# Filler products behind the last parts of w2, one eviction on another engine, and the flag's sums at a later place

## The chip, the cores and the metric

The kernel runs on one core of one Trainium2 chip. The metric is device time in microseconds (us) of one execution. Engines are named as in the profile: PE is TensorE (PEld its weight loads), DVE is VectorE, ACT is ScalarE, POOL is GpSimd, SP is SyncE, which issues all DMAs here.

## What is computed

The reference chains three layers over 4608 tokens (8 sequences of 576, 512 features): an attention through 32 memory slots, a soft mixture of 8 experts, and a last layer whose weights come as float64.

```python
x = attention(q, k, v, phi)                 # (4608, 512)
logits = x @ moe_phi                        # 32 slots
d = softmax(logits, over tokens); slot_input = d.T @ x
for e in range(8):                          # 4 slots per expert
    slot_out[e] = relu(slot_input[e] @ w1[e]) @ w2[e]
c = softmax(logits, over slots)
x = c @ slot_out
h = x @ w_in                                # 512 -> 2048
g = h - tanh(h)
out = g @ w_out                             # 2048 -> 512
```

The kernel replaces the last layer by a low-order form in the slot weights. A validity flag is computed beside it; where the flag says that the form would not be accurate enough, a general branch at the end recomputes the layer. With these inputs the branch is not taken into the general part.

## The kernel before

Every instruction stands in an order written out by hand. Two strings, `ORDER` for the attention and `TAIL` for all behind it, name small operations; the kernel emits them in that order, and each engine gets its own instructions in the order in which they are emitted. Only semaphores between engines move the time at which they run. All loads and stores are issued by SyncE: loads in one fixed sequence, each as soon as the page of SBUF that it overwrites has been given back.

The part that the change touches, with the names in `TAIL`:

- `a2.0` to `a2.15` and `a2.b` (function `a2_half`, line 1299): sixteen parts of w2, 1 MB each, multiplied as they land. Each part is 8 matrix products of 32 x 256, in four column groups of TensorE, accumulated in two PSUM banks. A float32 product counts as two instructions in the trace, so a part is x16 there. Each part that is done gives its page back, and a load of w_out follows into it.
- `nB`, `D2` (lines 1211, 1215): a small product of the validity flag between `a2.13` and `a2.14`.
- `so`, `sT`, `sC` (lines 1328 to 1338): the result of w2 is copied by ScalarE and VectorE, turned by four products and copied again.
- `ft0` to `ft3` (line 1352): the slot outputs times the decoded w_in, 32 x 256 products into four banks named `hS`; `hs` copies them (line 1364), `st` turns them (line 1371, tile `hp`).
- `tt`, `hc`, `gs`, `gz`, `G` (lines 1387 to 1415): powers of the result, and the factor tiles `G` on VectorE.
- `da`, `db`, `dc` (lines 950, 954, 958): three VectorE passes that turn a part of w_in or w_out from float64 words into float32; `ck` (line 964, ScalarE) sums what the flag needs; `rd` (line 1238) rounds.
- `L`, `M`, `or`, `Ra`, `Rb`, `Rc`, `Rd` (lines 1437 to 1501): the two halves' right-hand sides `R`, from `G`, w_out and the rows.
- `k0.b`, `u0.b`, then `k1.b`, `u1.b` for b from 0 to 17 (lines 1527, 1545): the output products of the first and of the second half of the columns, and their evictions from PSUM. A last letter V or A says whether VectorE or ScalarE evicts. Four banks take turns. Two evictions fill a transfer of 512 KB; the first and last of a half are 256 KB.
- `fs` (lines 1556 to 1559): four VectorE sums of the flag. `fB`, `fm`, `fw`, `fo`, `fb` (lines 1564 to 1585) finish the flag at the very end; all engines load it and branch (line 1601).

In `TAIL` of before, `fs` stands behind `u0.13A`; on VectorE that is behind the last decoding pass (`dc.wout.6`) and ahead of `u0.14V`.

Of the kernel before, what the change touches and what calls it, by code (L numbers as in the profile page):

```python
# [189 lines left out]
q3 h1.2 q4 h1.3 q5 ck.win.1 mh1 h1.4 h1.5 h1.6 h1.7 ms r0 cB r1 hT q6 dc da.win.5 rl z1 z0 sp0 sq0 cT sq2 tp0 sp1 a2.0  # L190
tp1 tc1 a2.1 tc0 tp2 stk db.win.5 a2.2 da.win.4 sq3 sq1 tp3 a2.3 da.win.6 tc2 lg0 tc3 tp4 tp5 lg1 a2.4 lg3 a2.5
db.win.4 tc5 lg2 da.win.7 tc4 a2.6 dc.win.5 z2 z3 cX a2.7 db.win.6 sp2 sp3 tp6 a2.8 da.wout.0 tp7 da.wout.1 tc7 a2.9
tc6 tp8 dc.win.4 db.wout.0 dc.win.6 ck.win.5 tc8 n3 tp9 nT n5 a2.10 tp10 db.wout.1 tc9 db.win.7 tp11 a2.11 ck.win.6
dc.win.7 ck.win.4 dc.wout.0 a2.12 a2.13 nB dc.wout.1 D2 a2.14 rd.0A a2.15 ck.win.7 a2.b so0 so1 sT0 sT1 sC0 sC1 ft0
tc10 da.wout.2 db.wout.2 ft1 rd.1A ft3 mgz dc.wout.2 hs0A st0 tc11 hs1A st1 ck.wout.0 tt0 da.wout.3 hc0 db.wout.3 ft2
gs0 gz0 G0.0 G0.1 da.wout.4 hs3A hs2A rd.2A ck.wout.2 st3 M0.0 st2 tt1 dc.wout.3 L01.1 L00.1 L01.0 gs1 hc1 gz1 rd.3P
L00.0 M0.1 M0.3 ck.wout.1 ck.wout.3 M0.2 o40A G1.1 G1.0 ss0 db.wout.4 L00.3 dc.wout.4 or0 ss1 Ra00A Ra01A L00.2 L01.2
Rb000A Rc00 L01.3 Rb001A Rb010A rd.4P k0.0 Rc01 da.wout.5 db.wout.5 k0.1 da.wout.6 k0.2 u0.0A k0.3 Rd00 Rd01 u0.2A
u0.1A u0.3A k0.4 M1.0 k0.5 k0.6 k0.7 u0.5A u0.4V k0.8 k0.9 u0.6A k0.10 Rb011A da.wout.7 L11.0 u0.7A db.wout.7 k0.11
u0.8A u0.9A k0.12 u0.10A L10.0 dc.wout.7 k0.13 M1.3 k0.14 u0.12A db.wout.6 dc.wout.5 u0.11A k0.15 dc.wout.6 k0.16  # L200
rd.6P u0.13A fs M1.1 k0.17 rd.5A M1.2 L10.1 u0.14V u0.17V ck.wout.7 o41A rd.7P L10.2 or1 u0.15A u0.16A L10.3 L11.2
Ra10V Rb100A Rc10 k1.0 Ra11V Rb101V Rc11 u1.0A Rd10 k1.1 k1.2 k1.3 k1.4 u1.1A ck.wout.5 k1.5 u1.2V u1.3V k1.6 u1.4V
L11.3 L11.1 u1.5A k1.7 u1.6V k1.8 u1.7V Rb110A k1.9 Rb111A Rd11 k1.10 u1.8A k1.11 k1.12 ck.wout.4 u1.9V u1.12A u1.10V
k1.13 u1.11V u1.13V k1.14 u1.14V k1.15 fB k1.16 k1.17 ck.wout.6 u1.16V fm fw fo fb u1.15A u1.17A
"""

ORDER = """
# [22 lines left out]
def tile_kernel(  # L230
# [13 lines left out]
    NP, P, NI, H, M = phi.shape[0], 128, 9, kv.shape[2], phi.shape[3] // kv.shape[2]  # L244
# [19 lines left out]
    mm = nc.tensor.matmul  # L264
# [3 lines left out]
    ident = cst.tile([P, P], F32, name="ident")  # L268
# [30 lines left out]
    def view(off, shape, dtype=F32):  # L299
        n = 1  # L300
        for d in shape[1:]:
            n *= d
        o, e, t = [x for x in lots if x[0] <= off][-1]
        assert off % 4 == 0 and off + 4 * n <= e, (off, shape)
        v = t[0 : shape[0], (off - o) // 4 : (off - o) // 4 + n]
        if dtype != F32:
            v = v.bitcast(dtype)
        if len(shape) > 2:
            names = "abcdefg"[: len(shape) - 1]
            v = v.rearrange(  # L310
                f"p ({' '.join(names)}) -> p {' '.join(names)}", **{c: d for c, d in zip(names[:-1], shape[1:-1])}
            )
        return v
# [103 lines left out]
    for w in PLAN.split():  # L417
        n, p = w.split(":")
        n, j = n.split(".")
# [438 lines left out]
    def op(name):  # L858
        def keep(f):
            T[name] = f  # L860
            return f

        return keep
# [14 lines left out]
    @op("ms0")  # L878
    def _():
        G.memset(siM, 0.0)  # L880
# [111 lines left out]
    def bank(j, name):  # L992
        return ps.tile([P, 512], F32, tag=f"bank{j}", name=name)
# [8 lines left out]
    n3 = sc_[:, 360 : 360 + NP]  # L1002
    n4 = sc_[0:NP, 364:366]
    n5 = sc_[0:NP, 368 : 368 + B].rearrange("p (r b) -> p r b", r=NP)
    D2 = sc_[:, 376 : 376 + B]
# [15 lines left out]
    dc = view(13 * PG, [P, NP, NI, NSL])  # L1021
# [269 lines left out]
    a2 = []  # L1291
# [52 lines left out]
    hS, hp = {}, {}  # L1344

    def feat_ops(k):
        @op(f"ft{k}")
        def _():
            hS[k] = bank(2 + k, "hS").rearrange("p (a x) -> p a x", a=2)
            for g in (2 * k, 2 * k + 1):  # L1350
                for kc in range(4):
                    mm(  # L1352
                        hS[k][32 * kc : 32 * kc + 32, g % 2],
                        soT[:, kc],
                        wf[g][:, kc],
                        start=True,
                        stop=True,
                    )

        for e_, c_ in (("V", V.tensor_copy), ("A", A.copy)):  # L1360

            @op(f"hs{k}{e_}")
            def _(c_=c_):
                c_(hSs[k], hS[k])

        @op(f"st{k}")
        def _():
            if k // 2 not in hp:
                hp[k // 2] = bank(6 + k // 2, "hp")[:, 0 : 8 * XW].rearrange("p (c x) -> p c x", x=XW)
            for c in range(4):  # L1370
                mm(
                    hp[k // 2][:, 4 * (k % 2) + c],
                    hSs[k][:, c // 2, (c % 2) * P : (c % 2) * P + P],
                    stkx,
                    start=True,
                    stop=True,
                )

    for k in range(4):
        feat_ops(k)  # L1380

    def curve_ops(k):
        c = slice(8 * k, 8 * k + 8)

        @op(f"tt{k}")
        def _():
            A.activation(out=tt_[:, c], in_=hp[k][:, :, NSL:], func=AF.Square)

        @op(f"hc{k}")
        def _():  # L1390
            A.copy(hc[:, c], hp[k][:, :, NSL:])

        @op(f"ss{k}")
        def _():
            A.activation(out=ss[:, c], in_=hp[k][:, :, 0:NSL], func=AF.Square)

        @op(f"gs{k}")
        def _():

            t = tt_[:, c]  # L1400
            V.scalar_tensor_tensor(out=gs[:, c], in0=t, scalar=-1.5, in1=t, op0=ALU.add, op1=ALU.mult)

        @op(f"gz{k}")
        def _():
            t = tt_[:, c]
            G.tensor_scalar(out=g2[:, c], in0=t, scalar1=-2.0 / 15.0, scalar2=1.0 / 3.0, op0=ALU.mult, op1=ALU.add)
            G.tensor_tensor(out=g2[:, c], in0=g2[:, c], in1=t, op=ALU.mult)
            G.tensor_tensor(out=gz[:, c, 0:B], in0=hc[:, c], in1=g2[:, c], op=ALU.mult)

        for j in range(2):  # L1410

            @op(f"G{k}.{j}")
            def _(j=j):
                b = slice(4 * j, 4 * j + 4)
                V.tensor_tensor(
                    out=curves(f"G{k}")[:, :, b],
                    in0=hp[k][:, :, 0:NSL].unsqueeze(2).to_broadcast([P, 8, 4, NSL]),
                    in1=gs[:, c, b].unsqueeze(3).to_broadcast([P, 8, 4, NSL]),
                    op=ALU.mult,
                )  # L1420
# [88 lines left out]
    n = 0  # L1509
# [174 lines left out]
```

## Time and profile before

| | us |
|---|---|
| median of 3 runs | 243.46 (242.02 to 244.72) |
| the profiled execution, its own time | 245.09 |
| span of its trace | 243.1 |
| busy in the span: PE, DVE, ACT, POOL | 179.4, 162.3, 99.0, 77.8 |
| DMA: moved, mean rate | 93.56 MB, 385 GB/s |

All times below are counted from the start of the span. The own time is 2.0 us more than the span, and the profiled execution is 1.6 us above the median of the runs.

### The profile page before, as it was taken

What the parts mean: (1) busy time and instruction counts of PE and PEld (TensorE: products, weight loads), DVE (VectorE), ACT (ScalarE), POOL (GpSimd) and SP (SyncE); (2) the same over time, 40 slices, a digit from 0 to 9 for tenths busy, and PEclk for the clock granted to TensorE, in tenths of its full rate; (3) what the DMA queues carried; (4) which work ended last, traced back from release to release, by engine and by line L of the source; (5) the groups of instructions that cost most, each with busy time, mean ns of one, the idle gap of its engine ahead of it and who ended that gap; (6) DMA issues with size and microseconds to landing.
All of it is one profiled execution on the core that took longest, in us unless ns stands there. A gap on an engine that the chain in (4) does not pass through costs nothing.

```text
span 243.1 us, 6355 instructions
## 1 busy us (share of the span) xinstructions
PE 179.4 (74%) x2657; PEld 126.3 (52%) x2657; DVE 162.3 (67%) x246; ACT 99.0 (41%) x192; POOL 77.8 (32%) x139
## 2 busy tenths in 40 slices
PE   0368299886998998857975986991757799878920
PEld 0255287665677777645552326550323467665720
DVE  1594649962587954862968999433496279999940
ACT  2131610851545355352341160120433359786930
POOL 4001148876573774331021034760000005404000
PEclk9999959999999999995599997699789679999975
DMA  6999999999999999999999999999999992086993
GB/s 248 425 414 417 422 419 416 415 417 420 420 416 409 422 421 423 419 425 427 431 426 417 406 418 430 425 426 429 423 426 425 426 426 96 21 358 269 393 419 113
DMA packets 17459, 93.56 MB, mean 385 GB/s; under 512 B 1936, under 2 KB 2064, under 8 KB 10768
## 3 DMA queue, kind: packets, MB, share of 16 engines
q1 hardware_dynamic: 17424, 93.09, 92.5%
q8 instruction: 23, 0.38, 0.6%
q14 instruction: 12, 0.10, 0.1%
HBM read 83.64 MB, written 9.44 MB: 383 GB/s over the span
## 4 chain that ended last, share of the span: by engine, by line
PE 32%; DVE 28%; DMA 23%; issue 5%; ACT 5%; POOL 3%; SPq 0%; DVEq 0%; ACTq 0%
DMA main<-in_w_dram 11%; DMA main<-in_q_dram 5%; PE yp L649 5%; DMA main<-in_kv_dram 5%; PE sc L722 4%; PE a L1299 3%; PE kvm L525 3%; DVE main L954 2%; DMA phiM<-in_moe_phi_dram 2%; PE lg L786 2%; PE pa L768 2%; PE hS L1352 2%; DVE main L958 2%; DVE last L737 2%; PE L L1437 2%
## 5 line engine op out<-in xcount | busy, mean ns | idle before, releaser
L722 PE MATMUL sc<-side,main 128*64 128x64 f32 x576 | 20.9, 232 | 8.6 <-DMA main<-in_q_dram 4.2
L525 PE MATMUL kvm<-main 128*32 128x129 f32 (+1 forms) x640 | 22.9, 309 | 3.5 <-ACT main L514 2.9
L1299 PE MATMUL a<-main,last 128*32 128x256 f32 x256 | 19.7, 444 | 7.8 <-DMA main<-in_w_dram 7.8
L722 PEld LDWEIGHTS sc<-side,main 128*64 128x64 f32 x576 | 19.1, 145 | 10.7 <-issue 6.8
L755 POOL TENSOR_TENSOR side<-side 128x192 f32<-128x192 f32 (+3 forms) x33 | 18.2, 552 | 12.4 <-ACT side L743 10.3
L525 PEld LDWEIGHTS kvm<-main 128*32 128x32 f32 (+1 forms) x640 | 18.4, 124 | 7.0 <-ACT main L514 3.7
L964 ACT ACTIVATE main<-main 128x1024 f32<-128x1024 f32 x16 | 18.7, 1178 | 4.7 <-DVE main L958 3.4
L737 DVE TENSOR_REDUCE last<-sc 128x24 f32<-128x768 f32 x12 | 11.4, 951 | 13.0 <-PE sc L722 12.9
L777 ACT COPY side<-pa 128x384 f32<-128x384 f32 x24 | 11.5, 478 | 19.1 <-PE pa L768 19.0
L950 DVE TENSOR_SCALAR main<-main 128x1024 uint32<-128x1024 uint32 x12 | 9.0, 746 | 14.8 <-issue 8.2
L1299 PEld LDWEIGHTS a<-main,last 128*32 128x32 f32 x256 | 7.8, 121 | 15.6 <-DMA main<-in_w_dram 9.4
L954 DVE SCALAR_TENSOR_TENSOR main<-main 128x1024 uint32<-128x1024 uint32 x12 | 14.9, 1248 | 0.1
L958 DVE SCALAR_TENSOR_TENSOR main<-main 128x1024 uint32<-128x1024 uint32 x12 | 14.4, 1221 | 0.1
L1527 PE MATMUL ot<-R,dcT 128*128 128x256 f32 x72 | 12.7, 301 | 1.5 <-DVE main L1545 0.8
L763 POOL TENSOR_TENSOR last<-last 128x768 f32<-128x768 f32 x6 | 8.9, 1482 | 14.9 <-DVE last L760 14.9
L786 PE MATMUL lg<-last,side 128*64 128x32 f32 x288 | 11.6, 236 | 2.1 <-ACT side L777 1.9
L1184 ACT CAST dcT<-pc 128x384 fp32r<-128x384 f32 x12 | 5.4, 483 | 18.8 <-PE pc L1179 18.8
L786 PEld LDWEIGHTS lg<-last,side 128*64 128x64 f32 x288 | 10.5, 152 | 3.9 <-ACT side L777 2.1
L1253 PE MATMUL h1p<-main,side 128*32 128x512 f32 x96 | 10.5, 593 | 2.5 <-DVE side L935 2.5
L1545 ACT COPY main<-ot 128x512 f32<-128x512 f32 x22 | 11.6, 603 | 1.2 <-PE ot L1527 1.0
L1527 PEld LDWEIGHTS ot<-R,dcT 128*128 128x128 f32 x72 | 9.7, 188 | 4.6 <-DVE main L1545 1.6
L763 POOL TENSOR_TENSOR side<-side,last 128x768 f32<-128x768 f32 x6 | 9.7, 1624 | 6.0 <-DVE last L760 5.9
(194 smaller groups left out, 375.4 us busy)
## 6 DMA issues: line engine op xcount, KB each, us to landing
main<-in_w_dram SPq DMA_DIRECT2D x28, 1024.0 KB, 13.9
main<-in_kv_dram SPq DMA_DIRECT2D x36, 516.0 KB, 11.8
main<-in_q_dram SPq DMA_DIRECT2D x12, 768.0 KB, 12.6
main<-in_w_in_dram SPq DMA_DIRECT2D x8, 1024.0 KB, 18.8
main<-in_w_out_dram SPq DMA_DIRECT2D x8, 1024.0 KB, 12.1
out_dram<-main SPq DMA_DIRECT2D x16, 512.0 KB, 4.6
main<-in_phi_dram SPq DMA_DIRECT2D x4, 1152.0 KB, 11.6
side<-in_w_dram SPq DMA_DIRECT2D x4, 1024.0 KB, 16.8
```

Source lines behind the costliest of these rows:

```text
L525: mm(kvp[pr][32 * h : 32 * h + 32, b, hq * HD : hq * HD + HD], x["ph"][r, n, 32 * (4 * hq + h) : 32 * (4 * hq + h) + 32], t[r, 4 * hq + h] ...
L649: mm(x["yp"][64 * (i % 2) : 64 * (i % 2) + 64, 0:256], x["d2"][:, i].rearrange("p b s -> p (b s)"), ats[pr][:, t0 + i], start=(i < 2), sto ...
L722: mm(scv[64 * bb : 64 * bb + 64, ii, hq, h2], qT[:, hq, ii, bb, 64 * h2 : 64 * h2 + 64], bds[pr % 2][:, h2, bb, hq], start=True, stop=True,)
L737: V.tensor_reduce(out=x["rm"][:, :, 0], in_=x["scv"], op=ALU.max, axis=AX.X)
L755: G.tensor_tensor(out=d, in0=a[:, :, 0:w], in1=a[:, :, w : 2 * w], op=ALU.add)
L763: G.tensor_tensor(out=x["atv"], in0=x["atv"], in1=x["sm"].to_broadcast([P, 8 * n, M]), op=ALU.mult)
L786: mm(lgp[pr][64 * bb : 64 * bb + 64, i * NSL : (i + 1) * NSL], x["aT"][:, hq, ii, 64 * bb : 64 * bb + 64], vps[pr][:, bb, hq], start=(hq = ...
L954: V.scalar_tensor_tensor(out=lo, in0=lo, scalar=29, in1=X, op0=ALU.logical_shift_right, op1=ALU.bitwise_xor)
L958: V.scalar_tensor_tensor(out=X, in0=hi, scalar=3, in1=lo, op0=ALU.logical_shift_left, op1=ALU.bitwise_xor)
L964: A.activation(out=t, in_=t, func=AF.Square, scale=2.0**-56, accum_out=big[:, j : j + 1])
L1299: mm(a2[j][32 * fj : 32 * fj + 32], h1M[:, f0 + fj, 32 * e : 32 * e + 32], w[:, fj, 256 * j : 256 * j + 256], start=(e2 == 0), stop=(e2 == ...
L1527: mm(pts[h, b][:, HM * t : HM * t + HM], rounded("dcT")[:, (NI * pr + i) * P : (NI * pr + i + 1) * P], curves(f"R{h}")[:, pr // 2, pr % 2] ...
```

## The change

Three things change; nothing else does.

- New operations `warm4`, `warm5`, `warm6`: 4, 5 or 6 products of the identity with itself, 128 x 128 by 128 columns, float32, into the first 128 columns of the bank that `ft0` overwrites later. Nobody reads them. `warm4` stands behind `a2.11`, `warm5` behind `a2.12` and again behind `a2.13`, `warm6` behind `a2.14`: 20 products.
- `u0.4V` becomes `u0.4A`: one eviction of the first half moves from VectorE to ScalarE.
- `fs` moves from behind `u0.13A` to behind `u1.4V`, into the evictions of the second half.

```diff
-tc6 ... tp11 a2.11 ck.win.6
-dc.win.7 ck.win.4 dc.wout.0 a2.12 a2.13 nB dc.wout.1 D2 a2.14 rd.0A a2.15 ck.win.7 a2.b so0 so1
+tc6 ... tp11 a2.11 warm4
+ck.win.6 dc.win.7 ck.win.4 dc.wout.0 a2.12 warm5 a2.13 warm5 nB dc.wout.1 D2 a2.14 warm6 rd.0A a2.15 ck.win.7 a2.b so0
...
-k0.6 k0.7 u0.5A u0.4V k0.8
+k0.6 k0.7 u0.5A u0.4A k0.8
...
-rd.6P u0.13A fs M1.1
+rd.6P u0.13A M1.1
...
-k1.6 u1.4V
-L11.3 L11.1 u1.5A
+k1.6 u1.4V fs L11.3 L11.1 u1.5A
...
+    def warm_op(n):
+
+        @op(f"warm{n}")
+        def _():
+            if 0 not in hS:
+                hS[0] = bank(2, "hS").rearrange("p (a x) -> p a x", a=2)
+            for _ in range(n):
+                mm(hS[0][:, 0, 0:P], ident, ident, start=True, stop=True)
+
+    for n in (4, 5, 6):
+        warm_op(n)
```

The first place is TensorE from the part `a2.12` on. `a_1733` and `a_1734` are the two banks of w2's result, so two rows are one part; `nB` is the flag's small product, `sp` the turning of the result. Before:

```order
L1299 MATMUL a_1733<-main,last 32x256 x4
L1299 MATMUL a_1734<-main,last 32x256 x4
L1299 MATMUL a_1733<-main,last 32x256 x4
L1299 MATMUL a_1734<-main,last 32x256 x4
L1211 MATMUL nB<-U_all,ones 128x8
L1299 MATMUL a_1733<-main,last 32x256 x4
L1299 MATMUL a_1734<-main,last 32x256 x4
L1299 MATMUL a_1733<-main,last 32x256 x4
L1299 MATMUL a_1734<-main,last 32x256 x4
L1334 MATMUL sp<-stk,main 128x32 x4
```

Now, from `warm4` (rows `hS<-ident`) to the first half of `a2.15`:

```order
L1391 MATMUL hS<-ident 128x128 x4
L1300 MATMUL a_1733<-main,last 32x256 x4
L1300 MATMUL a_1734<-main,last 32x256 x4
L1391 MATMUL hS<-ident 128x128 x5
L1300 MATMUL a_1733<-main,last 32x256 x4
L1300 MATMUL a_1734<-main,last 32x256 x4
L1391 MATMUL hS<-ident 128x128 x5
L1212 MATMUL nB<-U_all,ones 128x8
L1300 MATMUL a_1733<-main,last 32x256 x4
L1300 MATMUL a_1734<-main,last 32x256 x4
L1391 MATMUL hS<-ident 128x128 x6
L1300 MATMUL a_1733<-main,last 32x256 x4
```

The filler products stand between the parts, ahead of the part that may have to wait for its data; the flag's product comes behind the second group of five.

The second place is VectorE in the decoding of w_out's last parts during the first half's evictions. Line 1545 (`main<-ot`) is the eviction `u0.4V`. Before:

```order
L950 TENSOR_SCALAR main<-main 128x1024
L1545 COPY main<-ot 128x512
L950 TENSOR_SCALAR main<-main 128x1024
L954 SCALAR_TENSOR_TENSOR main<-main 128x1024
L958 SCALAR_TENSOR_TENSOR main<-main 128x1024
L954 SCALAR_TENSOR_TENSOR main<-main 128x1024
L958 SCALAR_TENSOR_TENSOR main<-main 128x1024 x2
```

Now (line numbers of the new file are higher by one here):

```order
L951 TENSOR_SCALAR main<-main 128x1024 x2
L955 SCALAR_TENSOR_TENSOR main<-main 128x1024
L959 SCALAR_TENSOR_TENSOR main<-main 128x1024
L955 SCALAR_TENSOR_TENSOR main<-main 128x1024
L959 SCALAR_TENSOR_TENSOR main<-main 128x1024 x2
```

The eviction between the two passes of line 950 has gone; on ScalarE it stands behind `u0.5A`.

The third place is VectorE behind the last decoding pass. Lines 1556 to 1559 are `fs`, `R` is the second half's right-hand side, and `main<-ot` are evictions. Before:

```order
L1556 TENSOR_REDUCE U_all<-main 128x16
L1557 TENSOR_REDUCE U_all<-U_all 128x1
L1558 TENSOR_SCALAR U_all<-U_all 128x1
L1559 TENSOR_REDUCE U_all<-main 128x8
L1545 COPY main<-ot 128x512 x2
L1481 CAST R_2077<-orep 64x256
L1496 TENSOR_TENSOR R_2077<-orep,R_2077 32x256
L1481 CAST R_2077<-orep 64x256
L1489 TENSOR_SCALAR R_2077<-L 64x256
L1496 TENSOR_TENSOR R_2077<-orep,R_2077 32x256
L1545 COPY main<-ot 128x512 x11
```

Now:

```order
L1559 COPY main<-ot 128x512 x2
L1495 CAST R_2097<-orep 64x256
L1510 TENSOR_TENSOR R_2097<-orep,R_2097 32x256
L1495 CAST R_2097<-orep 64x256
L1503 TENSOR_SCALAR R_2097<-L 64x256
L1510 TENSOR_TENSOR R_2097<-orep,R_2097 32x256
L1559 COPY main<-ot 128x512 x3
L1570 TENSOR_REDUCE U_all<-main 128x16
L1571 TENSOR_REDUCE U_all<-U_all 128x1
L1572 TENSOR_SCALAR U_all<-U_all 128x1
L1573 TENSOR_REDUCE U_all<-main 128x8
L1559 COPY main<-ot 128x512 x8
```

The four sums stand behind the third eviction of the second half on VectorE, with eight evictions behind them.

## Rows read from the trace of the kernel before

**Rows 1.** Page, granted TensorE clock in 40 slices of 6.08 us.

```profile
PEclk9999959999999999995599997699789679999975
```

**Rows 2.** Windows of 1 us: busy time by engine, granted clock (PEclk), DMA share, GB/s.

```profile
190.00:191.00 1.00, 1.00 (x16) 0.37 (x9) 0.00 (x0) 0.21 (x1) 0.00 (x0) 0.58 1.07 451
...
197.00:198.00 1.00, 1.00 (x18) 0.38 (x10) 0.96 (x2) 0.73 (x2) 0.00 (x0) 1.00 1.05 434
```

**Rows 3.** Timeline of TensorE, 150 to 205 us: start, length, instructions, [idle before].

```profile
160.82 3.66 PE L1299 MATMUL a<-main,last 128*32 128x256 f32 x64
...
182.33 2.40 PE L1299 MATMUL a<-main,last 128*32 128x256 f32 x32
184.99 1.07 PE L1299 MATMUL a<-main,last 128*32 128x256 f32 x16 [0.26 <-DMA main<-in_w_dram]
...
187.42 1.07 PE L1299 MATMUL a<-main,last 128*32 128x256 f32 x16 [1.04 <-DMA main<-in_w_dram]
189.85 1.69 PE L1299 MATMUL a<-main,last 128*32 128x256 f32 x16 [1.36 <-DMA main<-in_w_dram]
191.47 1.92 PE L1334 MATMUL sp<-stk,main 128*128 128x32 f32 x8
193.32 3.91 PE L1352 MATMUL hS<-last,U_all 128*32 128x256 f32 x32
...
198.02 1.98 PE L1371 MATMUL hp<-stkx,main 128*128 128x40 f32 x16
...
200.93 1.08 PE L1371 MATMUL hp<-stkx,main 128*128 128x40 f32 x8
```

**Rows 4.** Timeline of VectorE, 176 to 240 us.

```profile
191.66 0.42 DVE L1328 COPY main<-a 128x256 f32<-128x256 f32 x1 [5.08 <-PE a L1299]
...
197.41 1.23 DVE L954 SCALAR_TENSOR_TENSOR main<-main 128x1024 uint32<-128x1024 uint32 x1
200.29 0.23 DVE L1401 SCALAR_TENSOR_TENSOR main<-main 128x64 f32<-128x64 f32 x1 [1.65 <-ACT main L1387]
...
202.92 0.68 DVE L950 TENSOR_SCALAR main<-main 128x1024 uint32<-128x1024 uint32 x1
...
213.63 0.69 DVE L1545 COPY main<-ot 128x512 f32<-128x512 f32 x1
...
218.49 2.35 DVE L958 SCALAR_TENSOR_TENSOR main<-main 128x1024 uint32<-128x1024 uint32 x2
220.76 0.68 DVE L1556 TENSOR_REDUCE U_all<-main 128x16 f32<-128x512 f32 x1
...
222.06 1.28 DVE L1545 COPY main<-ot 128x512 f32<-128x512 f32 x2
...
225.66 6.95 DVE L1545 COPY main<-ot 128x512 f32<-128x512 f32 x11
...
233.94 0.16 DVE L1585 TENSOR_SCALAR U_all<-orep 128x1 int32<-128x1 f32 x1 [0.47 <-PE orep L1581]
```

**Rows 5.** Timeline of ScalarE, 176 to 240 us.

```profile
210.91 3.26 ACT L1545 COPY main<-ot 128x512 f32<-128x512 f32 x6 [0.35 <-PE ot L1527]
...
219.75 1.05 ACT L1238 CAST wr<-main 128x1024 fp32r<-128x1024 f32 x1 [1.62 <-DVE main L958]
```

**Rows 6.** Timeline of TensorE, 203 to 235 us.

```profile
222.75 0.60 PE L1471 MATMUL orep<-main,U_all 128*128 128x256 f32 x2
```

**Rows 7.** Issues on SyncE's queue, of a part of w_out and of the last outputs.

```profile
186.12 0.33 SPq L391 DMA_DIRECT2D main<-in_w_out_dram  x1
...
233.45 2.33 SPq L1548 DMA_DIRECT2D out_dram<-main  x2
```

**Rows 8.** Transfers of w_out, from issue to landing.

```profile
DMA to landing us min/median/max: 9.9/12.1/13.3
```

**Rows 9.** Windows of 5 us near the end.

```profile
225.00:230.00 5.00, 4.88 (x34) 4.09 (x32) 4.83 (x9) 4.70 (x9) 0.40 (x1) 1.00 1.01 404
...
235.00:240.00 5.00, 0.00 (x0) 0.00 (x0) 0.00 (x0) 0.00 (x0) 0.00 (x0) 0.50 0.76 290
```

More of the change, by code (lines that the diff above doesn't have):

```diff
@@ L192 @@
 db.win.4 tc5 lg2 da.win.7 tc4 a2.6 dc.win.5 z2 z3 cX a2.7 db.win.6 sp2 sp3 tp6 a2.8 da.wout.0 tp7 da.wout.1 tc7 a2.9
[L193 to L201, printed above, removed]
@@ L202 @@
-Ra10V Rb100A Rc10 k1.0 Ra11V Rb101V Rc11 u1.0A Rd10 k1.1 k1.2 k1.3 k1.4 u1.1A ck.wout.5 k1.5 u1.2V u1.3V k1.6 u1.4V
-L11.3 L11.1 u1.5A k1.7 u1.6V k1.8 u1.7V Rb110A k1.9 Rb111A Rd11 k1.10 u1.8A k1.11 k1.12 ck.wout.4 u1.9V u1.12A u1.10V
-k1.13 u1.11V u1.13V k1.14 u1.14V k1.15 fB k1.16 k1.17 ck.wout.6 u1.16V fm fw fo fb u1.15A u1.17A
+tc6 tp8 dc.win.4 db.wout.0 dc.win.6 ck.win.5 tc8 n3 tp9 nT n5 a2.10 tp10 db.wout.1 tc9 db.win.7 tp11 a2.11 warm4
+ck.win.6 dc.win.7 ck.win.4 dc.wout.0 a2.12 warm5 a2.13 warm5 nB dc.wout.1 D2 a2.14 warm6 rd.0A a2.15 ck.win.7 a2.b so0
@@ new lines @@
+so1 sT0 sT1 sC0 sC1 ft0 tc10 da.wout.2 db.wout.2 ft1 rd.1A ft3 mgz dc.wout.2 hs0A st0 tc11 hs1A st1 ck.wout.0 tt0
+da.wout.3 hc0 db.wout.3 ft2 gs0 gz0 G0.0 G0.1 da.wout.4 hs3A hs2A rd.2A ck.wout.2 st3 M0.0 st2 tt1 dc.wout.3 L01.1
+L00.1 L01.0 gs1 hc1 gz1 rd.3P L00.0 M0.1 M0.3 ck.wout.1 ck.wout.3 M0.2 o40A G1.1 G1.0 ss0 db.wout.4 L00.3 dc.wout.4
+or0 ss1 Ra00A Ra01A L00.2 L01.2 Rb000A Rc00 L01.3 Rb001A Rb010A rd.4P k0.0 Rc01 da.wout.5 db.wout.5 k0.1 da.wout.6
+k0.2 u0.0A k0.3 Rd00 Rd01 u0.2A u0.1A u0.3A k0.4 M1.0 k0.5 k0.6 k0.7 u0.5A u0.4A k0.8 k0.9 u0.6A k0.10 Rb011A
@@ new lines @@
+da.wout.7 L11.0 u0.7A db.wout.7 k0.11 u0.8A u0.9A k0.12 u0.10A L10.0 dc.wout.7 k0.13 M1.3 k0.14 u0.12A db.wout.6
+dc.wout.5 u0.11A k0.15 dc.wout.6 k0.16 rd.6P u0.13A M1.1 k0.17 rd.5A M1.2 L10.1 u0.14V u0.17V ck.wout.7 o41A rd.7P
+L10.2 or1 u0.15A u0.16A L10.3 L11.2 Ra10V Rb100A Rc10 k1.0 Ra11V Rb101V Rc11 u1.0A Rd10 k1.1 k1.2 k1.3 k1.4 u1.1A
+ck.wout.5 k1.5 u1.2V u1.3V k1.6 u1.4V fs L11.3 L11.1 u1.5A k1.7 u1.6V k1.8 u1.7V Rb110A k1.9 Rb111A Rd11 k1.10 u1.8A
+k1.11 k1.12 ck.wout.4 u1.9V u1.12A u1.10V k1.13 u1.11V u1.13V k1.14 u1.14V k1.15 fB k1.16 k1.17 ck.wout.6 u1.16V fm fw
@@ L205 @@
+fo fb u1.15A u1.17A
 """
@@ L1348, in _ @@
         def _():
-            hS[k] = bank(2 + k, "hS").rearrange("p (a x) -> p a x", a=2)
+            if k not in hS:
+                hS[k] = bank(2 + k, "hS").rearrange("p (a x) -> p a x", a=2)
             for g in (2 * k, 2 * k + 1):
```

## The prediction

> **What bounds the kernel now.** I read the page's clock row first, then windows of 1 us where it dips, then the timelines of TensorE, VectorE and ScalarE through that place, and last SyncE's issues and the DMA windows at the end. The clock row dips at slices 31 and 32, 188 to 201 us [rows 1]. Slice 30, 182 to 188 us, has nine tenths or more of full speed [rows 1]; the window from 190 has a granted 0.58, which puts a fall from 2.4 to 1.2 GHz near 190.2, and the one from 197 is back at 1.00 [rows 2]. In the 5 us ahead of it TensorE worked little: it had the parts of w2 one by one as they landed, 1.07 us each, with 0.26 to 1.36 us of waiting for the next [rows 3]. Then it ran the last part (1.69 us where a warm one takes 1.07), the turning `sp` (1.92) and two thirds of `hS` (3.91 for 32 instructions) at the low clock [rows 3].
>
> What this costs the kernel is read from VectorE. It waits 5.08 us for w2's result, decodes wout.2 and part of wout.3 until 198.64 (197.41 + 1.23), then waits 1.65 us for the powers that come out of `hS` and `hp`, at 200.29 [rows 4]. From there to 232.6 its timeline has no hole of note: factors, decoding, sums, evictions. So from 200 to 221 VectorE sets the pace. Behind it come the transfers of the output: the engines' last eviction on VectorE ends at 232.61 (225.66 + 6.95) [rows 4], but from 225 to 230 the DMA share is already 1.01 at 404 GB/s, and after 235, with no engine busy, data still moves at 290 GB/s [rows 9]. SyncE's last issue ends at 235.78 (233.45 + 2.33) [rows 7]; only then does SyncE come to its branch on the flag.
>
> **Part 1, the filler products.** No identity product of this size stands in the trace. A 128-row product of this kind is in `hp`: 16 instructions in 1.98 us, 8 in 1.08, so 0.9 us more for 8, 0.113 each, 0.225 us for a float32 product of two instructions [rows 3]. From below: the parts of w2, 64 instructions in 3.66 and 16 in 1.07, 0.054 each, 0.11 a product, since four column groups work side by side; from above: `sp` at the low clock, 8 in 1.92, 0.48 a product [rows 3]. I take 0.225, the nearest in shape, and 0.87 us for a part of w2 in a stream (16 x 0.054). The 20 products are then 4.5 us, against 2.66 us of waiting (0.26 + 1.04 + 1.36) that they can lie in.
>
> TensorE then runs like this. `a2.11` ends near 183.7 (half of the 2.40 us row, its first part at the low clock [rows 3]). `warm4` to 184.6, `a2.12` to 185.5, `warm5` to 186.6, `a2.13` to 187.5, `warm5` to 188.6, `nB` to 188.8, `a2.14` to 189.7, `warm6` to 191.0, `a2.15` with `a2.b` to 191.9, 192.1 with the drain. Before it was 191.54 (189.85 + 1.69): 0.6 late. At the high clock `sp` takes half, but it is held by two copies, so it ends near 193.4, as before. `hS` starts there and takes 2.1 us for its first 32 instructions (two groups of 16 at 1.07) and not 3.91; the last 16 and `hp` were warm for most of their time. The powers so come near 198.3, 1.7 us sooner than now, and VectorE, which still ends its decoding at 198.64, goes on at 198.8 and not 200.29: **-1.5 us**, at most 1.65, the length of its wait. With a product at 0.11 the last part would not be late at all, and VectorE would gain up to 2.4 (the wait and 0.8 from an earlier decoding); at 0.48 the last part would come 6 us late and the end some 4 us.
>
> A later `a2.13` gives its page back later: w_out's load into it is issued at 186.12 [rows 7], 1.4 us later now. Loads of w_out take 9.9 to 13.3 us to land [rows 8], so it lands by 200.9, and VectorE asks for it at 201.4 (202.92 less 1.5 [rows 4], where its first pass stands now). I count nothing; without that cover it would be the 1.4 us.
>
> Here the trace and a rule of the notes differ. Of the idle times of TensorE between 184.7 and 190.2 the longest is 1.36 us [rows 3], and yet the clock fell. The Trainium skill, page "TensorE: Matmul & The Clock Gate", section "Why this matters for your kernels", says that the throughput drops where idle gaps between bursts are longer than any gap here; by that rule the fillers have nothing to save and only their delay is left. The trace does not bear it out: many short waits did it too.
>
> **Part 2, the eviction.** On VectorE it took 0.69 us at 213.63, between decoding passes that follow one another: **-0.69**. ScalarE takes 0.54 for one (3.26 for six) [rows 5]. It has 1.62 us of idle time behind the first half's evictions, ahead of 219.75 [rows 5], so that hides it; without it ScalarE's next cast would be 0.54 late. VectorE's last decoding pass then ends at 218.65 and not at 220.84 (218.49 + 2.35 [rows 4]): -2.2 in all.
>
> **Part 3, the flag's sums.** They stand from 220.76 to 222.06, 1.30 us [rows 4], ahead of two evictions that end at 223.34. Right there the second half's right-hand side can start, because TensorE's product for it (`orep`) ends at 223.35 (222.75 + 0.60) [rows 6]. That chain (last decoding pass, two groups of products, `orep`) takes 2.5 us by itself, so taking the sums out of it gives nothing: VectorE will stand idle there for about 1.2 us. It only brings the evictions `u0.14` and `u0.17` forward by 3.4 us. Behind the third eviction of the second half the 1.30 us are paid in a row of evictions without holes (11 in 6.95, 0.63 each): from there VectorE is only 0.9 ahead of now (2.2 - 1.3), and the flag, now at 233.94 [rows 4], comes at 233.0.
>
> What is late then? Transfers. A pair of evictions is 0.524 MB, 1.30 us at 404 GB/s; the whole half 4.72 MB, 11.7 us. The evictions of the half need 8 us. So the queue falls behind and most of a late eviction is hidden. The fourth lot waits for the first eviction behind the sums, 0.9 ahead where the queue would be 2.4 ahead, and the queue runs dry for 0.6 us. The transfers so end about **1.7 us** sooner, SyncE's last issue and branch with them; the other engines' branch follows the flag, **0.9 us** sooner. The end needs both: I take **-1.4**. The profiled execution would go from 245.09 (243.1 of span and 2.0 around it) to 243.7. It lies 1.6 above the median of the runs; from that median, 243.46, I forecast 242.1.
>
> **Rivals.**
> - *All of it arrives.* The fillers cost less than I take, or the fourth lot is not late since the queue has more in it. Then the end follows the second half, 2.2 to 2.9 us sooner: 240.9. For it: data still moves after 235, when every engine is done [rows 9]. Against it: 4.5 us of fillers do not fit in 2.66 us.
> - *The clock falls all the same.* `sp` waits for copies and its products have few columns; now, at the low clock from 190.2 with TensorE busy throughout, it took until 197 to come back [rows 2]. If it falls at 190.2, `warm6` and the last part run at the low clock: the last part ends at 193.7, 2.2 late, and with the clock up again at 197.0 VectorE goes on 1.25 later than now. Less 0.69 that is +0.6 for the transfers and +1.9 (with the sums) for the flag, +1.3 for the end: 244.8, slower than before. Were all of `hS` at the low clock it would be +2.9, 246.4. It decides as soon as the clock is at half when `hS` starts. Against it: TensorE has work for all but some 0.8 us up to `hS`, far more than ahead of the fall now.
> - *Most runs keep the clock without fillers.* By the Trainium skill's rule above all of them would. Only one execution has a profile, and the median is 1.6 us below it. In a run that keeps it the last part would end at 190.9 and the fillers make it 192.1: 1.2 late, +0.5 after the eviction's 0.69, +1.8 for the flag, +1.2 at the end: 244.7. For it: the median. Against it: the profile's own cost could be that difference, and the waits for w2 come from the DMA rate, the same in each run.
>
> **How the numbers follow.** The forecast has 0.50 (its own range 241.2 to 243.0), all of it arrives 0.20, the clock falls anyway 0.13, the clock was kept 0.12, and 0.05 that nothing can be seen (243.5). Within 1% is 241.0 to 245.9, about what a measurement of this kernel can tell from no change. Faster by more: 0.20 and the lower edge of the forecast, 0.06: 0.26. Slower by more: the part of the second rival that loses all of `hS` to the low clock, 0.05, and 0.03 for fillers near their upper price: 0.08. The rest is 0.66. For the range I leave out less than a tenth at each side: 240.0, where the first rival has cheap fillers as well, to 244.9, just above the middle of the two slower rivals.
>
> **What would show it.** In the new trace the granted clock should be 1.00 from 184 to beyond 200; the fillers should be 40 instructions of some 0.11 us, and the last part should end near 192.1. VectorE's wait of 1.65 us ahead of line 1401's first row should be gone, with that row near 198.8; the last decoding pass should end near 218.7, an idle time of about 1 us stand ahead of the second half's casts, and the flag come near 233.0. The forecast is wrong if the clock is at 0.5 in `hS`, if the last part comes more than 1.5 us late, if w_out's parts land too late for VectorE, or if the DMA share falls well below 1 behind the sums.

## The result and the profile after

The change is slower: 245.30 us median of 20 runs (243.96 to 246.99) against 243.79 of 20 runs of before (242.02 to 247.03). The ratio is 1.0075, 95% interval 1.0048 to 1.0101, some 1.8 us; the medians are 1.5 apart. The forecast was 242.1 with a range of 240.0 to 244.9: the sign is wrong and the time lies outside. The profiled execution took 246.11 us, its span is 243.9. A ratio here compares only the runs that are no more than 1.5% above the fastest of their kernel; of the 12 runs of one experiment below (`evict_only`) that leaves six, and there I go by the median of all.

The clock did what was forecast, but for its start. Windows of 1 us of the kernel after, with busy time by engine, granted clock (1.00 is 2.4 GHz, 0.50 is 1.2), DMA share and GB/s:

```profile
184.00:185.00 1.00, 1.00 (x16) 0.29 (x8) 1.00 (x2) 0.00 (x0) 0.00 (x0) 0.50 1.00 410
...
190.00:191.00 1.00, 1.00 (x10) 0.96 (x9) 0.00 (x0) 0.00 (x0) 0.00 (x0) 1.00 1.01 426
...
196.00:197.00 1.00, 1.00 (x15) 0.62 (x18) 0.72 (x2) 1.00 (x2) 0.00 (x0) 1.00 0.97 410
```

It is at 1.00 in the windows from 190 and 196, where [rows 2] had 0.58 and where `hS` ran at the low clock. But it is still at 0.50 in the window from 184. The timeline of TensorE (line 1300 is w2's parts, 1391 the fillers, 1335 `sp`, 1354 `hS`):

```profile
183.47 1.94 PE L1300 MATMUL a<-main,last 128*32 128x256 f32 x16
185.33 1.19 PE L1391 MATMUL hS<-ident 128*128 128x128 f32 x8
186.45 1.07 PE L1300 MATMUL a<-main,last 128*32 128x256 f32 x16
187.45 1.38 PE L1391 MATMUL hS<-ident 128*128 128x128 f32 x10
188.77 1.07 PE L1300 MATMUL a<-main,last 128*32 128x256 f32 x16
189.77 1.38 PE L1391 MATMUL hS<-ident 128*128 128x128 f32 x10
191.08 0.38 PE L1212 MATMUL nB<-U_all,ones 4*128 4x8 f32 x2
191.39 1.07 PE L1300 MATMUL a<-main,last 128*32 128x256 f32 x16
192.39 1.60 PE L1391 MATMUL hS<-ident 128*128 128x128 f32 x12
193.93 1.07 PE L1300 MATMUL a<-main,last 128*32 128x256 f32 x16
195.11 1.13 PE L1335 MATMUL sp<-stk,main 128*128 128x32 f32 x8
196.18 2.09 PE L1354 MATMUL hS<-last,U_all 128*32 128x256 f32 x30
```

TensorE waits for no data from here to `sp`, and there the delay comes in: `hS` takes 2.09 us for 30 instructions and not 3.91 for 32 [rows 3], but the last part of w2 starts at 193.93 and not at 189.85. It ends at 195.0, 3.5 us after 191.54. VectorE's timeline, with its idle time in brackets:

```profile
195.13 0.42 DVE L1329 COPY main<-a 128x256 f32<-128x256 f32 x1 [3.47 <-ACT main L1329]
...
196.42 0.72 DVE L951 TENSOR_SCALAR main<-main 128x1024 uint32<-128x1024 uint32 x1
...
200.34 1.23 DVE L955 SCALAR_TENSOR_TENSOR main<-main 128x1024 uint32<-128x1024 uint32 x1
201.55 0.23 DVE L1415 SCALAR_TENSOR_TENSOR main<-main 128x64 f32<-128x64 f32 x1
...
219.02 2.36 DVE L959 SCALAR_TENSOR_TENSOR main<-main 128x1024 uint32<-128x1024 uint32 x2
221.41 1.29 DVE L1559 COPY main<-ot 128x512 f32<-128x512 f32 x2
223.90 0.43 DVE L1495 CAST R<-orep 64x256 fp32r<-64x256 f32 x1 [1.21 <-PE orep L1485]
...
226.18 1.89 DVE L1559 COPY main<-ot 128x512 f32<-128x512 f32 x3
228.10 0.69 DVE L1570 TENSOR_REDUCE U_all<-main 128x16 f32<-128x512 f32 x1
...
229.39 4.88 DVE L1559 COPY main<-ot 128x512 f32<-128x512 f32 x8
...
235.47 0.16 DVE L1599 TENSOR_SCALAR U_all<-orep 128x1 int32<-128x1 f32 x1 [0.47 <-PE orep L1595]
```

VectorE gets w2's result at 195.13 (191.66 in [rows 4]) and starts to decode wout.2 at 196.42, 2.85 later than before, where that row was

```profile
193.57 0.68 DVE L950 TENSOR_SCALAR main<-main 128x1024 uint32<-128x1024 uint32 x1
```

From there to the evictions it has no wait: line 1415 (`gs`, line 1401 before) follows its last pass at once, at 201.55. So the 1.65 us wait has gone, as forecast, but the row stands 1.26 later than before (200.29), not 1.5 sooner. The eviction's 0.69 brings the last decoding pass back to 221.38 against 220.84, the idle time of 1.21 us ahead of the right-hand side's cast is there as forecast, the sums stand from 228.10 among the evictions, and the flag comes at 235.47 against 233.94. On ScalarE the moved eviction took the room that was there; its idle time ahead of the cast fell from 1.62 [rows 5] to 0.39:

```profile
220.28 1.05 ACT L1239 CAST wr<-main 128x1024 fp32r<-128x1024 f32 x1 [0.39 <-DVE main L959]
```

The windows of 5 us at the end have a DMA share of 0.86 and 0.88. Before it was 1.01 [rows 9] and, in the next window, 1.00. After:

```profile
225.00:230.00 5.00, 4.29 (x28) 3.52 (x28) 4.81 (x12) 4.19 (x9) 0.72 (x2) 1.00 0.86 351
230.00:235.00 5.00, 3.29 (x18) 2.42 (x18) 4.92 (x13) 3.68 (x7) 0.00 (x0) 1.00 0.88 361
235.00:240.00 5.00, 0.38 (x2) 0.30 (x2) 0.16 (x1) 0.00 (x0) 0.00 (x0) 0.66 0.89 351
```

Before:

```profile
230.00:235.00 5.00, 2.26 (x14) 1.59 (x12) 3.52 (x11) 2.99 (x7) 0.00 (x0) 0.95 1.00 408
```

Two things could so be the cause: the fillers, which make the last part late, or the sums, behind which the transfers run short.

### The profile page after: what moved, and what is told of

Same layout as the page of the kernel before. It is cut to its first block, busy times and chain, and to the rows that moved or that the text cites. A ratio compares the mean times of both kernels' runs of the same rounds, so it can differ in the third digit from the quotient of the medians.

```text
span 243.9 us, 6436 instructions
## 1 busy us (share of the span) xinstructions
PE 186.3 (76%) x2697; PEld 128.7 (53%) x2697; DVE 161.5 (66%) x245; ACT 99.5 (41%) x193; POOL 78.1 (32%) x139
## 4 chain that ended last, share of the span: by engine, by line
DVE 32%; PE 31%; DMA 21%; issue 5%; ACT 4%; POOL 3%; SPq 0%; DVEq 0%; ACTq 0%
DMA main<-in_w_out_dram 8%; DMA main<-in_q_dram 5%; PE sc L723 5%; PE a L1300 5%; DMA main<-in_kv_dram 5%; DVE main L955 4%; DVE main L959 3%; PE lg L787 3%; PE pa L769 3%; PE kvm L526 3%; DMA main<-in_phi_dram 2%; PE pc L1180 2%; PE yp L650 2%; DVE main L951 2%; DVE main L1559 2%
## 5 line engine op out<-in xcount | busy, mean ns | idle before, releaser
L1300 PE MATMUL a<-main,last 128*32 128x256 f32 x256 | 21.7, 477 | 4.8 <-DMA main<-in_w_dram 4.8
L526 PE MATMUL kvm<-main 128*32 128x129 f32 (+1 forms) x640 | 21.3, 296 | 3.1 <-ACT main L515 2.9
L526 PEld LDWEIGHTS kvm<-main 128*32 128x32 f32 (+1 forms) x640 | 17.1, 118 | 6.3 <-ACT main L515 3.7
L1541 PE MATMUL ot<-R,dcT 128*128 128x256 f32 x72 | 13.4, 306 | 2.2 <-DVE main L1559 0.7
L1254 PE MATMUL h1p<-main,side 128*32 128x512 f32 x96 | 13.4, 725 | 2.1 <-DVE side L936 2.1
L1559 ACT COPY main<-ot 128x512 f32<-128x512 f32 x23 | 12.2, 601 | 1.9 <-PE ot L1541 1.0
```

The source lines that it names most:

```text
L526: mm(kvp[pr][32 * h : 32 * h + 32, b, hq * HD : hq * HD + HD], x["ph"][r, n, 32 * (4 * hq + h) : 32 * (4 * hq + h) + 32], t[r, 4 * hq + h] ...
L1300: mm(a2[j][32 * fj : 32 * fj + 32], h1M[:, f0 + fj, 32 * e : 32 * e + 32], w[:, fj, 256 * j : 256 * j + 256], start=(e2 == 0), stop=(e2 == ...
L1541: mm(pts[h, b][:, HM * t : HM * t + HM], rounded("dcT")[:, (NI * pr + i) * P : (NI * pr + i + 1) * P], curves(f"R{h}")[:, pr // 2, pr % 2] ...
L1559: c_(obs[h, n][:, o : o + 2].rearrange("p a x -> p (a x)"), pts[h, b])
```

## The experiments

The theory: the fillers cost more than the waits hold, and the whole loss comes from there. The rival: the moved sums cost it, and the fillers are neutral. All kernels compute the full output; only words of `TAIL` and the numbers of fillers differ. Each edit is shown shortened (`...` stands for words left out), against the change, and for `evict_only`, `sums_only` and `sums_mid` against the kernel before.

**fill_only.** The fillers without the two other parts.

```diff
-... u0.5A u0.4A k0.8 ... u0.13A M1.1 ... u1.4V fs L11.3
+... u0.5A u0.4V k0.8 ... u0.13A fs M1.1 ... u1.4V L11.3
```

> The 20 filler products alone; eviction and sums stand as before. Theory of the delay: the products cost more than the waits hold (about 0.26 us each instead of 0.225), w2's last part ends near 195 us, VectorE starts its decoding of wout.2 near 196.3 and has no wait ahead of line 1415; from there all is late by 1.0 to 1.5 us, and the time is 1.0 to 1.8 us above before. Theory of the sums (the moved sums alone make the change slower): the same as before within 0.5 us, or up to 1.5 us below it. Theory of chance (the clock came up late in the one profiled run): last part near 192.1 and a gain of about 1 us.

Measured: 245.25 us median of 12, before 244.41 (35 runs on that chip); ratio 1.0068 (1.0037 to 1.0100). The fillers alone are as slow as the whole change. Its TensorE timeline:

```profile
183.71 1.10 PE L1300 MATMUL a<-main,last 128*32 128x256 f32 x16
184.73 1.16 PE L1391 MATMUL hS<-ident 128*128 128x128 f32 x8
...
186.82 1.38 PE L1391 MATMUL hS<-ident 128*128 128x128 f32 x10
...
193.30 1.07 PE L1300 MATMUL a<-main,last 128*32 128x256 f32 x16
```

Here the clock came back sooner than in the kernel after (`a2.11`, at 183.71, took 1.10 us and not 1.94), and the last part still starts at 193.30, 3.4 us late. So the one late clock was not the cause. A group of five takes 1.31 us (186.82 to 188.13, where the next part begins). And with the sums where they stood, the transfers at the end are not short of work, though the loss is the same:

```profile
225.00:230.00 5.00, 4.82 (x34) 4.11 (x33) 4.80 (x9) 4.06 (x9) 0.79 (x2) 1.00 1.00 401
```

**evict_only.** The eviction on ScalarE, no fillers, sums as before.

```diff
-u0.5A u0.4V k0.8
+u0.5A u0.4A k0.8
```

> The eviction u0.4 on ScalarE alone; no products are emitted and the sums stand as before. All theories: VectorE's last decoding pass 0.7 us sooner than before; with that on the path, 0.4 to 0.8 us below before; if ScalarE's evictions become the bound there instead, no change.

Measured: 244.65 median of 12 (241.08 to 246.88) against 244.41. The gain that I expected can't be seen in the medians; the ratio of 0.9926 (0.9876 to 0.9977) rests on six runs. In the trace VectorE's last row of decoding begins at 218.10, 17.48 us after the first row of `gs` (line 1414 here) at 200.62; in [rows 4] it is 18.20 (200.29 to 218.49). So the 0.7 us are there; the runs spread too widely to show them.

**sums_only.** The sums behind `u1.4V`, no fillers, eviction as before.

```diff
-u0.13A fs M1.1 ... u1.4V L11.3
+u0.13A M1.1 ... u1.4V fs L11.3
```

> The flag's sums behind u1.4 alone; no products, eviction as before. Theory of the delay: the second half starts as before, the evictions behind the sums and the flag are 1.3 us later (flag near 235.2), DMA share below 0.9 behind the sums; time 0.5 to 1.3 us above before. Theory of the sums: the same mechanism carries the whole loss, 1.5 to 2 us above before.

Measured: 245.05 median of 12 against 244.41; ratio 1.0021 (0.9978 to 1.0065): between 0.5 us sooner and 1.6 later. The 1.5 to 2 us of the rival are hardly in that range, and it does not tell whether the place costs anything.

**no_fill.** The change without its fillers.

```diff
-a2.11 warm4 ... a2.12 warm5 a2.13 warm5 nB ... a2.14 warm6
+a2.11 ... a2.12 a2.13 nB ... a2.14
```

> The change without its products: eviction on ScalarE, sums behind u1.4. Theory of the delay: second half 0.7 us sooner, flag 0.6 us later than before; time within 0.6 us of before, and 1 to 1.8 us below the whole change. Theory of the sums: 1 us or more above before, as slow as the whole change within 0.5 us.

Measured: 243.34 median of 12 against 244.41; ratio 0.9951 (0.9917 to 0.9985), faster than before by more than the 0.6 us that I allowed. With the rival it would have been as slow as the whole change. Its profiled execution kept the clock without a filler. Windows of 1 us and one of 5, TensorE's and VectorE's timelines:

```profile
190.00:191.00 1.00, 0.52 (x12) 0.35 (x16) 0.00 (x0) 0.00 (x0) 0.00 (x0) 1.00 0.99 418
...
194.00:195.00 1.00, 1.00 (x25) 0.78 (x20) 0.97 (x2) 0.72 (x2) 0.00 (x0) 1.00 1.01 426
...
225.00:230.00 5.00, 3.99 (x21) 2.97 (x19) 4.93 (x11) 4.19 (x9) 0.00 (x0) 0.86 0.79 323
```

```profile
182.95 3.74 PE L1299 MATMUL a<-main,last 128*32 128x256 f32 x48
...
188.05 1.07 PE L1299 MATMUL a<-main,last 128*32 128x256 f32 x16 [1.04 <-DMA main<-in_w_dram]
190.48 1.07 PE L1299 MATMUL a<-main,last 128*32 128x256 f32 x16 [1.36 <-DMA main<-in_w_dram]
191.67 1.13 PE L1334 MATMUL sp<-stk,main 128*128 128x32 f32 x8
```

```profile
196.86 1.23 DVE L954 SCALAR_TENSOR_TENSOR main<-main 128x1024 uint32<-128x1024 uint32 x1
198.10 0.22 DVE L1414 SCALAR_TENSOR_TENSOR main<-main 128x64 f32<-128x64 f32 x1
```

The last part ends at 191.55, as in before, the clock is at 1.00 in `hS`, and VectorE goes on at 198.10, 2.2 us sooner than before. This is what the fillers were to bring, and here chance brought it. It is the third rival's mechanism: some runs keep the clock. Of the five profiled executions without fillers (before, `evict_only`, `sums_only`, `no_fill`, `sums_mid`) this one alone kept it through `hS`. The DMA share behind the sums is 0.79 here, lower than in the change, and the kernel is faster than before: a dip there is not by itself a loss.

**fill_fit.** Eight fillers, sized to the waits: eviction and sums as before.

```diff
-a2.11 warm4 ... a2.12 warm5 a2.13 warm5 nB ... a2.14 warm6
+a2.11 ... a2.12 warm1 a2.13 warm3 nB ... a2.14 warm4
```

> 8 filler products alone, sized to the waits: none behind a2.11, 1 behind a2.12, 3 behind a2.13, 4 behind a2.14 (2.1 us at 0.26 each, in 2.66 us of waits). Theory of the delay: the last part of w2 starts within 0.4 us of before (near 190.2); if the clock holds to 197 VectorE goes on 1 to 2 us sooner and the time is 0.5 to 1.5 us below before. Rival (few products do not hold the clock, or it is held in many runs without them): same as before within 0.5 us.

Measured: 243.14 median of 12 against 243.87 (22 runs); ratio 0.9966 (0.9931 to 1.0000). The clock holds through `hS`, and 12 fillers fewer are 2.1 us by the medians (245.25 to 243.14) and 2.5 by the ratios. With 20 the fillers lose; with 8 alone they gain a little or nothing, as the interval reaches 1.0000.

**fill_double.** Forty fillers (8, 10, 10, 12), eviction and sums as before.

> 40 filler products alone (8, 10, 10, 12). Theory of the delay: every further product is paid in full, 20 x 0.26 = 5.2 us; last part of w2 near 200 us, time 4.5 to 5.5 us above the run with 20 alone, some 6 to 7 above before. If the products lie in waits, or the end is set by the transfers or by something the products bring besides their time: less than 3 us more.

Measured: 249.65 median of 5 (249.51 to 250.11); ratio 1.0231 (1.0190 to 1.0272).

```profile
186.62 1.07 PE L1300 MATMUL a<-main,last 128*32 128x256 f32 x16
187.62 2.50 PE L1391 MATMUL hS<-ident 128*128 128x128 f32 x20
190.05 1.07 PE L1300 MATMUL a<-main,last 128*32 128x256 f32 x16
...
197.67 1.07 PE L1300 MATMUL a<-main,last 128*32 128x256 f32 x16
```

The last part starts at 197.67, 4.4 us behind that of `fill_only` (193.30), and the median is 4.4 above (4.0 by the ratios): each further filler is paid in full. It also gives the price apart from the group's: ten products take 2.43 us (187.62 to 190.05), five 1.32 (187.45 to 188.77 in the kernel after), so 0.22 for a further product and 0.2 for each group. The 5.2 us that I expected were too much for that reason.

**sums_mid.** No fillers, eviction on ScalarE, sums in VectorE's idle time ahead of the right-hand side.

```diff
-u0.13A fs M1.1 ... u0.14V u0.17V ck.wout.7
+u0.13A M1.1 ... u0.14V u0.17V fs ck.wout.7
```

> No products; eviction u0.4 on ScalarE; the sums behind u0.17 and ahead of the second half's right-hand side, where VectorE waited 1.2 us for the product orep in the runs with the sums moved. Theory that the sums are paid among the second half's evictions: here they are nearly free, flag and second half both 0.6 us sooner than before, time 0.6 to 1.2 us below before and 0.3 to 0.8 below the run without products that has the sums behind u1.4. Rival (the transfers hide the sums there): same as that run.

Measured: 244.72 median of 12; ratio 1.0027 (0.9985 to 1.0069). A miss: no gain. The runs fall in two groups, four from 241.6 to 243.3 and eight from 244.3 to 245.2. The groups are not the clock kept and the clock lost: the profiled run, 243.25, is of the faster four, and its clock fell too, behind w2's last part:

```profile
192.00:193.00 1.00, 1.00 (x10) 0.74 (x13) 0.46 (x2) 1.00 (x3) 0.00 (x0) 0.52 1.05 442
```

What sets them apart is not shown, and with such a spread a place of the sums can't be judged.

**best_fit and fit_mid.** The same kernel, run twice: eight fillers, eviction on ScalarE, sums behind `u0.17V`.

> 8 filler products as in fill_fit, eviction on ScalarE, sums behind u0.17. If the three add up: 1.2 to 2.5 us below before. If the few products bring nothing: as the run without them.

> The best version again (8 products, eviction on ScalarE, sums behind u0.17): 0.8 to 1.4% below before, and the lowest of the four.

Measured: 241.79 median of 6 against 243.87, ratio 0.9896 (0.9856 to 0.9935); and 242.25 median of 12 against 244.33, ratio 0.9931 (0.9890 to 0.9971). It is faster than before. `sums_mid`, which is this kernel without its fillers, stood at 1.0027 (0.9985 to 1.0069) beside `best_fit`: there eight fillers were worth 1.3%. Timeline of TensorE in `fit_mid`, then VectorE's row that waited before:

```profile
183.38 3.11 PE L1299 MATMUL a<-main,last 128*32 128x256 f32 x32
186.42 0.49 PE L1390 MATMUL hS<-ident 128*128 128x128 f32 x2
...
187.84 0.94 PE L1390 MATMUL hS<-ident 128*128 128x128 f32 x6
...
190.02 1.16 PE L1390 MATMUL hS<-ident 128*128 128x128 f32 x8
191.11 1.07 PE L1299 MATMUL a<-main,last 128*32 128x256 f32 x16
```

```profile
198.73 0.23 DVE L1414 SCALAR_TENSOR_TENSOR main<-main 128x64 f32<-128x64 f32 x1
```

The groups of fillers are 0.49 to 1.16 us long here, the last part starts at 191.11 (its end, 192.2, is 0.6 behind before), and VectorE goes on at 198.73, 1.6 sooner.

**fit_new and fit_old.** Eight fillers and the eviction on ScalarE; the sums behind `u1.4V` as in the change, or where they stood before.

> 8 products sized to the waits, eviction on ScalarE, sums behind u1.4 as in the change. Theory: paid among the second half's evictions; flag 1.3 us later than with the sums behind u0.17 and the transfers short of work behind them; time 0.6 to 1.3 us above that run, and still 0.5 to 1.2 us below before, so that the number of products alone turns the change from slower into faster. Rival (the transfers hide the sums): same as that run within 0.3 us.

> 8 products sized to the waits, eviction on ScalarE, sums where they stood before (ahead of u0.14). Theory: they lie beside the chain last decoding pass to orep (2.5 us), so the second half starts as with the sums behind u0.17; time within 0.4 us of that run. Rival (the sums hold up the second half there): 0.6 to 1.3 us above it.

Measured, on the chip of `fit_mid`: 242.53 for `fit_new` (ratio 0.9942, 0.9909 to 0.9975) and 242.41 for `fit_old` (0.9948, 0.9912 to 0.9984). The medians of the three places of the sums are within 0.3 us of each other, and each interval is some 0.9 us to either side. For `fit_old` the theory holds; for `fit_new` I expected 0.6 to 1.3 us above `fit_mid`, and that did not come; the rival, that the transfers hide the sums, fits better. Windows at the end of `fit_new`:

```profile
225.00:230.00 5.00, 3.92 (x23) 2.85 (x21) 4.93 (x11) 4.16 (x9) 0.00 (x0) 0.96 0.98 403
230.00:235.00 5.00, 1.68 (x7) 1.30 (x6) 1.91 (x8) 1.07 (x3) 0.00 (x0) 0.50 1.03 419
```

The share is 0.98 and 1.03 behind the sums: the transfers have enough to do. `fit_new` differs from the change in nothing but the number of fillers, 8 instead of 20, and is faster than before where the change is slower. `no_fill`, with none, is as fast (0.9951), so this pair shows the loss with 20, not a gain with 8.

**fill_evict.** The change with the sums where they stood.

> The change with its 20 products and its eviction, sums where they stood before. Theory of the delay: 0.4 to 0.8 us below the run with the products alone, 0.5 to 1.2 us above before; 2 to 2.8 us above the run with 8 products and the same sums. Rival (the sums alone make the change slower): below before.

Measured: 244.91 median of 12; ratio 1.0046 (1.0015 to 1.0077). Still slower than before, and 2.5 us above `fit_old` on the same chip, which has 8 fillers for its 20. The rival, by which it would have been below before, is out.

By place in the trace, over the profiled executions (us; the mean of each group, with its range):

| | last part of w2 ends | VectorE goes on (first `gs`) |
|---|---|---|
| no fillers, 4 kernels (without `sums_only`) | 191.6 (191.1 to 192.3) | 199.5 (198.1 to 200.6) |
| 8 fillers, 5 executions | 192.1 (191.6 to 193.0) | 198.7 (198.3 to 199.5) |
| 20 fillers, 3 kernels | 195.2 (194.4 to 196.2) | 201.7 (200.9 to 202.8) |

Twenty fillers make VectorE 2.2 us later; less 0.7 for the eviction that is 1.5, of a measured 1.8. The profiled run of `sums_only`, the second slowest of its twelve (246.62), has 193.4 and 201.6; with it the 2.2 would be 1.8.

## Why the prediction was wrong

**The fillers' sum (part 1) failed.** Its words were "191.9, 192.1 with the drain. Before it was 191.54 (189.85 + 1.69): 0.6 late". It was 3.5 late in the profiled execution and 3.6 in the mean of the groups. Two terms of it are shown by the rows.
- The size: I had 4.5 us for the fillers and 0.87 for a part in a stream. A further product does cost 0.22, as `hp` had it, but each group has 0.2 on top, and a part that stands alone between groups takes 1.0 (186.45 to 187.45). From the end of `a2.11` to the end of the last part I had 8.4 us; it took 9.7 (185.33 to 195.0), and 9.6 and 9.9 in `fill_only` and `fill_evict`.
- The start: I let the chain begin at 183.7, from the one execution before. In the kernel after TensorE was at the low clock until the window from 185, `a2.11` took 1.94, and the chain began at 185.33, 1.6 later. The one execution had an early start: its `a2.11` at 182.33 is the earliest of the 14 traces, the latest is at 184.56 (`fill_fit`). Before, a late start does less harm, because the parts wait for their data anyway. In `fit_mid` `a2.11` starts at 183.38, and with eight fillers the last part still ends only 0.6 later than before. With twenty there is no wait left, and every late start goes through to the end. The waits were a buffer, and I had counted them only as room for fillers.

I did write the main argument against myself, "4.5 us of fillers do not fit in 2.66 us", and used it only against the first rival.

The steps behind that sum held where the last part came in time. In `fit_mid` it ends at 192.2 (192.1 in the forecast) and VectorE goes on at 198.73 (198.8). `fit_new`, the change with fillers that fit, is 1.4 us below before by its ratio (0.9942), the forecast's own -1.4; that match is in part luck, since `no_fill` comes to nearly the same without any.

**Right in part 1:** the clock holds, `hS` takes 2.1 us, VectorE's wait of 1.65 us goes. My price for a filler was right for a product and wrong for a group. The w_out loads were not late for VectorE: it has no wait from 196.42 to 221.38. The load into `a2.13`'s page was issued at 189.90, 3.8 later than before and not 1.4, but landed in 7.8 us, at 197.7. "Many short waits did it too" was too strong: `no_fill` had the same two waits ahead of its last parts, 1.04 and 1.36 us, and kept the clock.

**The eviction (part 2) was right in the trace**: 0.7 us on VectorE and hidden on ScalarE. In the runs it is some 0.5 us, within the noise (1.0068 without it, 1.0046 with it, intervals that overlap).

**The sums (part 3) were right in mechanism** (the chain to `orep` hides them where they stood, VectorE idles 1.2 us there afterwards, the flag is later behind them). The price of -2.4 turning into -1.7 at the transfers is not shown: with eight fillers the medians of the three places differ by 0.3 us, but the intervals would hide a price of that size.

**The rivals.** "The clock falls all the same" did not happen in any trace with fillers. "Most runs keep the clock without fillers" was right that some do, one of five traces; how many runs do is not known. That takes away part of the gain, so the price had to be weighed against the mean over runs and not against the one profiled execution. The runs of before spread over 5.0 us (242.02 to 247.03), those of the change over 3.0 (243.96 to 246.99), of `fit_mid` over 3.3 (240.87 to 244.18) and the five of `fill_double` over 0.6. The clock can be a part of the spread of before. Every trace with fillers kept it; if their other runs did too, what spread is left has another source, which I can't tell from one trace each.

Not settled is how much the sums cost in the change itself, where the half starts later and the DMA share did fall to 0.86.

## What to carry to other kernels

Filler work that keeps a clock up has to be smaller than the waits that it lies in, with the price of each group counted, not of each product: 20 products alone lost some 1.7 us (ratio 1.0068) where 8 alone gained some 0.8 or nothing (0.9966, 0.9931 to 1.0000). Waits for data are also the buffer that absorbs an earlier delay, so filling them to the last leaves every late start on the path. And where the kernel before has a state that comes and goes from run to run, one profile shows one case of it: take the price of a fix from several executions.

## What the runs showed of the hardware

- A float32 product of 128 x 128 by 128 columns costs 0.22 us in a row of equal ones, and a group of them between products of another shape 0.2 us more (five took 1.32 us, ten 2.43).
- In the kernel before TensorE fell from 2.4 to 1.2 GHz near 190.2, behind two parts of 1.07 us and a small product with waits of 1.04 and 1.36 us. In `no_fill` the same parts with the same waits left it at 2.4 GHz, and in `sums_mid` it fell only near 192. The first rows of `hS` took 3.91 us for 32 instructions at the low clock and 2.09 for 30 at the high one, and VectorE went on at 200.29 and at 198.10.
